# Adjacent weight rows a partition and regrouped attention outputs in a two-layer decode step

## The chip, the cores and the metric

The kernel runs on one core of a Trainium2 chip. The core has a matrix engine (PE, with its weight loads listed as PEld), a vector engine (DVE), a scalar engine (ACT), GpSimd (POOL), a queue engine that issues the loads (SP), and sixteen DMA engines that carry them. The metric is device time in microseconds of one execution, and a version of the kernel is judged by the median of several. Before the change the median of three runs is 268.01 us; the three lie between 267.9 and 269.52.

## The reference

Two layers that share all weights are run on four batch rows of one token each. Each layer is attention over a cache, then a gated feed-forward block, both behind a layer norm and added to the residual.

```python
def _A_ref(x, k_cache, v_cache, wq, wo):          # x: 4 x 1 x 512
    q = (x @ wq).reshape(B, Sq, Hq, Dh)           # 32 query heads of 128
    k, v = repeat(k_cache, 4), repeat(v_cache, 4) # 8 key heads, 4096 positions
    p = softmax(einsum(q, k) * Dh ** -0.5)
    return (p @ v).reshape(B, Sq, Hq * Dh) @ wo   # wo: 4096 x 512
def _B_ref(x, w_gate, w_up, w_down):              # 512 x 1792, 1792 x 512
    return (gelu(x @ w_gate) * (x @ w_up)) @ w_down

x = x + _A_ref(layernorm(x), ...); x = x + _B_ref(layernorm(x), ...)
x = x + _A_ref(layernorm(x), ...); x = x + _B_ref(layernorm(x), ...)
```

All tensors are bf16. The key and value caches are 33.5 MB each for the four batch rows. Keys are read once and serve both layers; most values are read twice, some tiles stay on the chip between the layers.

## The kernel before

**Stages.** `attend_first` does the first layer's attention of batch row 0, `dense_first` its feed-forward block. Then, for each following row, `attend` works on two rows at once: the second layer's attention of the row before and the first layer's attention of its own row. `dense` does the feed-forward block of one row. At the end `attend_last` does the second layer's attention of the last row, and `dense_last` does the second feed-forward block for all four rows together. The order of the instructions is written out by hand (`tc.manual_schedule()`), and each engine runs its own in that order.

**Loads.** All of them are issued by SP on one queue. A key or value tile is 512 KB: 128 partitions of 16 cache positions (4 KB). In batch row 0 the first four heads are loaded whole, 1 MB with 8 KB a partition. Value tiles go through a ring of eight slots (`VRing`); a slot is free again when PE has used its tile, and SP waits for that. `load_wq` brings the query weights, one half for each group of four key heads; `load_rest` (L158 to L171) brings the output weights in four pieces, then gate, up and down. Before the change the row of `wo`, gate and up that lands in partition p of block k is row 128k + p of the matrix, so that each row is a run of its own: 1 KB for the output weights, 3.5 KB for gate and up. Down already comes as two adjacent rows a partition.

**Heads.** Eight key heads form two groups (`gx`, `gy`) of four; each serves four query heads (`rep`). Odd batch rows begin with the second group. `Values.step` multiplies one value tile with the softmax weights on PE. Where a head is `streamed`, DVE turns the sums from PSUM (`turn_v`, L799) and adds them up (`sum_v`, L806 and L807); else L680 scales them. `hold=True` leaves that for a later `flush`. The results stand in `OT_bf`, `OL_bf` (the last head of the first layer) or `OT2_bf` (second layer, all four rows): 128 partitions, one column for each query head.

**Output projection.** Most of it goes through `RowProj.heads` (L405), where the attention output is the stationary operand and a row block of `wo_sb` streams by, four heads at once in four quarters of the array. `RowProj.split` (ACT L412, DVE L413) takes the sums out of PSUM, and `onto` adds them into the bank of `OutProj`, which does the heads that come last with `wo_sb` as the stationary operand (L275). `heads = pairs(...)` lists the four pairs of key heads in the order in which they are finished. `busy` issues matmuls whose result nobody reads.

**The end.** In `attend_last` the value tiles 0 to 7 of the second group come last. Its step is: four tiles, two pairs of heads of `rows`, two tiles, the third pair, `split`, one tile, `proj` for one head, one tile, `onto`, `proj` for the last head. `dense_last` then takes the residual into rows through a matmul with the identity (`row`, L1440).

```python
vals.step(4)
rows.heads(heads[0], hp)
rows.heads(heads[1], hp)
vals.step(2)
rows.heads(heads[2], hp)
rows.split()
```

Of the kernel before, what the change touches and what calls it, by code (L numbers as in the profile page):

```python
# [15 lines left out]
P = 128  # L16

LN_EPS = 1e-5
QD = 4
# [12 lines left out]
ROWS_A = 8  # L32
UP_ROWS = 8


@with_exitstack
def kernel(
# [111 lines left out]
    def cache_tile(cache, b, kvh, t):  # L149
        if whole(b, kvh):  # L150
            return cache[b, kvh].rearrange("(p t c) d -> t p c d", t=NT, p=P)[t]
        return cache[b, kvh].rearrange("(t p c) d -> t p c d", t=NT, p=P)[t]

    def load_wq(g):
        n = HG * Dh
        dq.dma_start(out=wq_sb[g][:], in_=wq_dram[:, :, g * n:(g + 1) * n])

    def load_rest():  # L158
        n = Hq // 4
        for i in range(4):  # L160
            dq.dma_start(out=wo_sb[:, i * n:(i + 1) * n], in_=wo_dram[:, i * n:(i + 1) * n])  # L161
        dq.dma_start(out=wg_sb[:], in_=B_w_gate.rearrange("(k p) n -> p k n", p=P))
        dq.dma_start(out=wu_sb[:], in_=B_w_up.rearrange("(k p) n -> p k n", p=P))
# [110 lines left out]
    def mac(dst, lhsT, rhs, first, last):  # L274
        nc.tensor.matmul(dst, lhsT=lhsT, rhs=rhs, start=first, stop=last, skip_group_check=True)  # L275
# [51 lines left out]
    def down_rows(H_bf):  # L327
        return streamed("y2", KD, [(H_bf[:, c, :1], wd_sb[:, c]) for c in range(KF)])

# [46 lines left out]
    class OutProj:  # L376
# [8 lines left out]
        def heads(self, h0, n):  # L385
            for i in range(h0, h0 + n):
                for k in range(KD):
                    mac(self.full[:, k], wo_sb[:, i, k * P:(k + 1) * P],
                        wide(self.o(i), self.width),
                        self.n == 0 and k == 0, self.n == Hq - 1)  # L390
                self.n += 1

    class RowProj:
# [23 lines left out]
        def onto(self, proj):  # L417
            for x in self.parts:
                for k in range(KD):
                    mac(proj.full[:, k], x[:, k * P:(k + 1) * P], wide(self.pick, proj.width),  # L420
                        False, False)
# [63 lines left out]
    def down(nb, H_bf, whole):  # L485
        y = acc([KD, WIDE], "y2", whole)
        for c in range(KF):
            for k in range(KD):
                mac(y[:, k], wd_sb[:, c, k * P:(k + 1) * P], wide(H_bf[:, c, :]),
                    c == 0 and k == 0, c == KF - 1)  # L490
        return y[:, :, :nb]
# [318 lines left out]
    class Values:  # L810
        def __init__(self, layer, b, tiles, prob, dst, keeps=(), streamed=(), paired=(), sums=None, park=(),
                     last_bank=None, off_ot=False, last_width=WEIGHT):
# [71 lines left out]
        def unit(self, kvh):  # L884
            pair = [2 * (kvh // 2), 2 * (kvh // 2) + 1]
            alone = kvh in self.streamed and kvh not in self.paired
            return [kvh] if self.tiles[-1][0] in pair or alone else pair

        def scale(self, ot, unit, rden):
            n, s = len(unit), unit[0] % GH  # L890
            if unit[0] in self.streamed:
# [67 lines left out]
    def attend_first():  # L959
# [7 lines left out]
                      streamed=[h for h in range(Hkv) if h != last],  # L967
                      paired=[h for h in range(Hkv) if h // 2 != last // 2])
        ring.extend(1, b, one(b))
        load_wq(gx)  # L970
        keys.load_heads(GH)
        load_wq(gy)
# [5 lines left out]
        for k in range(KD):  # L978
            nc.tensor.transpose(xT_ps[:, k, :], x_bf[:B, k * P:(k + 1) * P], ident_bf[:B, :B])
        nc.vector.tensor_copy(out=xb[:, :, :B], in_=xT_ps[:])  # L980
# [3 lines left out]
        def q_first(g):  # L984
# [6 lines left out]
            center(q1_bf[:, g], q[:, :, :B], t, rstd1, B)  # L991

        q_first(gx)
        q_build(q1_bf[:, gx, :, b])
        sc1 = new_scores()
        for s in range(GH):
            keys.turn(NT)
            for t in range(NT):
                scores_of(sc1, gx, [(s, t)])
# [18 lines left out]
        prob1[gy] = (soft_swap(p0), soft_recip(soft_den(p0)))  # L1018
        vals.step(TG)
        assert vals.left() == 0  # L1020
        load_rest()
# [113 lines left out]
    def attend(b, qy, before, norm, early=None):  # L1135
# [13 lines left out]
                       sums={4: (ps_sc, "sc"), 5: (ps_sm, "sm"), 6: (ps_sc, "sc")},  # L1149
                       last_bank=lambda: ps_sm.tile([P, 2, WEIGHT], FP32, name="ot", tag="sm"))  # L1150

# [62 lines left out]
        vals1.step(3)  # L1214
        scores(sc1, gy, 1, last_alone)
        p0 = soft(sc1)
        vals1.step(3)
# [14 lines left out]
        vals1.step(2)  # L1232
        rows.heads(heads[1], hp)
        vals1.step(1)
        proj = OutProj(o1(b), 1)
        spare = proj.bank[:, KD * WEIGHT:]
        rows.heads(heads[2], rep)
        busy(3, spare)
        vals1.step(1)
        rows.heads(heads[2] + rep, rep)  # L1240
        rows.split()
        busy(5, spare)
        vals1.step(1)
        proj.heads(heads[3], rep)
        vals1.step(1)
        assert vals1.left() == 0
        rows.onto(proj)
        proj.n = Hq - rep
        proj.heads(heads[3] + rep, rep)
        return proj.y, late2  # L1250

    def attend_last(q_bf, norm, before, late):
# [7 lines left out]
                      paired=[h for h in range(Hkv) if h // 2 != tiles[-1][0] // 2],  # L1260
                      last_width=WIDE)
        sc2 = [new_scores(early=True)]
# [26 lines left out]
        for part in full:  # L1289
            nothing(part[:])  # L1290
        nc.scalar.preload_act_table_set("gelu_apprx_tanh_and_others")
        vals.step(4)
        rows.heads(heads[0], hp)
        rows.heads(heads[1], hp)
# [77 lines left out]
    def dense_last(y, full, squares):  # L1372
# [65 lines left out]

        def row(to, k, lhsT, rhs):
            nc.tensor.matmul(to[k * QS:k * QS + B], lhsT=lhsT, rhs=rhs, start=False, stop=True,  # L1440
                             skip_group_check=True)

        for x in (xb[:], xlo):
            for k in range(KD):
                row(xr, k, x[:, k, :B], ident_bf[:])

# [126 lines left out]
```

## Time and profile before

| what | value |
|---|---|
| median of three runs | 268.01 us (267.9 to 269.52) |
| profiled execution | 268.99 us |
| its span | 267.2 us |
| mean granted clock of PE | 0.866 of full speed |
| PE busy | 195.1 us, 73% of the span |
| DVE busy | 182.2 us, 68% |
| ACT busy | 66.0 us, 25% |
| DMA | 30732 packets, 103.05 MB, 386 GB/s in the mean |
| share of sixteen DMA engines taken by SP's loads | 95.7% |

The span is the profiled execution from its first to its last instruction; its own time is 1.8 us longer. Times of the timeline count from the start of the span. A wait in brackets behind a row is the time for which the engine stood idle just before it, with what ended it.

### The profile page before, as it was taken

How to read it: one execution, taken by the hardware profiler on the slowest of the kernel's cores; microseconds unless marked ns; L12 is line 12 of the kernel's file. 1: busy time of each engine (PE TensorE's matmuls, PEld its weight loads, DVE VectorE, ACT ScalarE, POOL GpSimd, SP SyncE). 2: the span in 40 equal slices, each digit the busy share in tenths (PEclk: the TensorE clock that was granted, in tenths of full speed). 3: DMA queues.
4: the chain of work that ended last, by engine and by line, in shares of the span. 5: the costliest groups of instructions: out<-in, count | busy, mean ns of one | idle time of the engine just before them, and what ended most of it. 6: DMA issues, size and time to landing. Idle time of an engine off the chain costs nothing.

```text
span 267.2 us, 8596 instructions
## 1 busy us (share of the span) xinstructions
PE 195.1 (73%) x3767; PEld 114.8 (43%) x3775; DVE 182.2 (68%) x448; ACT 66.0 (25%) x136; POOL 3.9 (1%) x10
## 2 busy tenths in 40 slices
PE   1396246544689796989678968787788687888884
PEld 1333123322255453557436245464363354553563
DVE  3385955451335899884776998746769996568773
ACT  1001001100222422032323520304136103044642
POOL 2000000000001000000000000000000000000001
PEclk9998555655597959799999985899999979999999
DMA  7999999999994999999999999999999999999940
GB/s 244 432 416 421 423 429 417 408 385 406 413 412 177 394 416 417 420 417 400 390 414 416 416 419 421 416 415 375 403 418 418 421 415 418 420 405 405 413 160 3
DMA packets 30732, 103.05 MB, mean 386 GB/s; under 512 B 2788, under 2 KB 7144, under 8 KB 29672
## 3 DMA queue, kind: packets, MB, share of 16 engines
q1 hardware_dynamic: 30672, 102.51, 95.7%
q8 instruction: 29, 0.48, 0.6%
q14 instruction: 7, 0.06, 0.1%
q10 hardware_dynamic: 24, 0.01, 0.0%
HBM read 102.50 MB, written 0.00 MB: 384 GB/s over the span
## 4 chain that ended last, share of the span: by engine, by line
DMA 51%; PE 21%; DVE 16%; SPq 6%; ACT 3%; issue 3%; DVEq 0%
DMA v_t<-in_A_v_cache_dram 25%; DMA kp<-in_A_k_cache_dram 8%; DMA kw<-in_A_k_cache_dram 8%; PE sc L592 6%; DMA wu_sb<-in_B_w_up_dram 5%; DMA kw<-in_A_v_cache_dram 4%; SPq L161 4%; DVE kp L537 3%; PE ot L859 3%; DVE kw L537 3%; PE y L275 3%; PE so L791 2%; PE q L309 1%; DVE q L315 1%; DVE qb L360 1%
## 5 line engine op out<-in xcount | busy, mean ns | idle before, releaser
L592 PE MATMUL sc<-kw,qb 128*32 128x512 bf16 x244 | 39.6, 446 | 5.2 <-DVE kw L537 2.2
L592 PE MATMUL sc<-kp,qb 128*32 128x512 bf16 x268 | 40.1, 450 | 1.0 <-DVE kp L537 0.2
L592 PEld LDWEIGHTS <-qb 128*32 128x32 bf16 x512 | 23.1, 104 | 39.6 <-issue 21.4
L537 DVE STREAM_TRANSPOSE kw<-kw 128x1024 f32<-128x1024 f32 x32 | 38.0, 1215 | 0.7 <-DMA kw<-in_A_k_cache_dram 0.6
L537 DVE STREAM_TRANSPOSE kp<-kp 128x1024 f32<-128x1024 f32 x32 | 36.7, 1199 | 0.0
L859 PE MATMUL ot<-pe,v_t 128*128 128x32 bf16 (+1 forms) x896 | 30.0, 184 | 5.6 <-DMA v_t<-in_A_v_cache_dram 2.8
L859 PEld LDWEIGHTS <-v_t 128*128 128x128 bf16 x896 | 27.7, 100 | 13.7 <-issue 7.4
L614 ACT ACTIVATE pe<-sc,nl 128x512 bf16<-128x512 f32 x8 | 5.5, 687 | 85.9 <-DVE pe L611 67.6
L791 PE MATMUL so<-v_t,pe 128*32 128x256 bf16 x304 | 15.0, 319 | 13.6 <-DMA v_t<-in_A_v_cache_dram 11.6
L799 DVE STREAM_TRANSPOSE so<-so 128x512 f32<-128x512 f32 (+1 forms) x23 | 13.8, 599 | 11.1 <-PE so L791 11.1
L791 PEld LDWEIGHTS <-pe 128*32 128x32 bf16 x320 | 9.1, 105 | 19.4 <-issue 12.5
L602 DVE TENSOR_REDUCE pe<-sc 128x1 f32<-128x512 f32 x12 | 8.3, 691 | 9.2 <-PE sc L592 9.1
L405 PE MATMUL yr<-wo_sb,OT_bf 128*2 128x512 bf16 (+1 forms) x120 | 10.7, 425 | 4.9 <-DMA wo_sb<-in_A_wo_dram 4.9
L647 PE MATMUL x<-pe,ident_bf 128*32 128x128 bf16 x192 | 5.4, 233 | 11.8 <-DVE pe L622 11.8
L647 PEld LDWEIGHTS <-ident_bf 128*32 128x32 bf16 x256 | 5.3, 100 | 16.1 <-issue 14.1
L791 PE MATMUL so<-v_t,pl 128*32 128x256 bf16 x192 | 9.4, 275 | 3.3 <-DMA v_t<-in_A_v_cache_dram 3.3
L650 ACT CAST pe<-x 128x512 bf16<-128x512 f32 x12 | 7.0, 586 | 17.4 <-PE x L647 17.4
L275 PE MATMUL q<-xb,wq_sb 128*128 128x5 bf16 (+1 forms) x192 | 5.7, 173 | 6.5 <-DMA wq_sb<-in_A_wq_dram 6.5
L353 PE MATMUL qe<-q_bf,ident_bf 128*32 128x16 bf16 (+1 forms) x272 | 5.7, 176 | 5.6 <-DVE q_bf L335 2.9
L622 DVE STREAM_TRANSPOSE pe<-pe 128x512 bf16<-128x512 bf16 x12 | 8.4, 696 | 1.1 <-ACT pe L614 1.1
L275 PEld LDWEIGHTS <-wo_sb 128*128 128x128 bf16 x160 | 7.6, 101 | 3.3 <-DMA wo_sb<-in_A_wo_dram 2.6
L482 PEld LDWEIGHTS <-ident_bf 128*128 128x128 bf16 x63 | 5.2, 99 | 8.7 <-issue 4.3
(172 smaller groups left out, 255.2 us busy)
## 6 DMA issues: line engine op xcount, KB each, us to landing
v_t<-in_A_v_cache_dram SPq DMA_DIRECT2D x89, 512.0 KB, 8.5
kp<-in_A_k_cache_dram SPq DMA_DIRECT2D x32, 512.0 KB, 9.9
kw<-in_A_k_cache_dram SPq DMA_DIRECT2D x24, 512.0 KB, 9.6
wq_sb<-in_A_wq_dram SPq DMA_DIRECT2D x2, 2048.0 KB, 7.7
kw<-in_A_k_cache_dram SPq DMA_DIRECT2D x4, 1024.0 KB, 11.6
v_t<-in_A_v_cache_dram SPq DMA_DIRECT2D x4, 1024.0 KB, 14.2
wo_sb<-in_A_wo_dram SPq DMA_DIRECT2D x4, 1024.0 KB, 12.0
wq_sb<-in_A_v_cache_dram SPq DMA_DIRECT2D x3, 1024.0 KB, 11.8
```

Of the source, the lines that this page charges most:

```text
L161: dq.dma_start(out=wo_sb[:, i * n:(i + 1) * n], in_=wo_dram[:, i * n:(i + 1) * n])
L275: nc.tensor.matmul(dst, lhsT=lhsT, rhs=rhs, start=first, stop=last, skip_group_check=True)
L405: nc.tensor.matmul(self.rows[j:j + x.shape[1]], lhsT=x, rhs=wo_sb[:, i], start=self.n < QD, stop=True, skip_group_check=True)
L537: nc.vector.transpose(out=words, in_=words)
L592: nc.tensor.matmul(sc[s * QS:(s + 1) * QS], lhsT=qb[:, w0:w0 + 2 * W], rhs=kt[:, :, be // 2, :, be % 2], start=(t == 0 and be == 0), stop= ...
L602: nc.vector.tensor_reduce(out=m, in_=sc.rearrange("p c j -> p (c j)"), axis=AX.X, op=ALU.min if norm else ALU.max)
L622: nc.vector.transpose(out=flat, in_=flat)
L647: nc.tensor.matmul(x[a * QS:(a + 1) * QS, s], lhsT=ident_bf[:, s * QS:(s + 1) * QS], rhs=pT[:, a], start=True, stop=True, skip_group_check ...
L650: nc.scalar.copy(out=pe, in_=x.rearrange("p s t c h -> p (s t c h)"))
L791: nc.tensor.matmul(ps[d, :NW * QS], lhsT=x[:, w:w + NW].rearrange("p c h -> p (c h)"), rhs=v[:, i:i + NW, d], start=first and i == 0, stop ...
L799: nc.vector.transpose(out=flat, in_=flat)
L859: nc.tensor.matmul(self.ot[:, s % 2], lhsT=v[:, i, :], rhs=wide(pe[:, s, t * CH + i, :], self.ot.shape[-1]), start=(done == 0 and i == 0), ...
```

## The change

The rows of a weight matrix that land in one partition become adjacent rows in memory.

- Gate and up: partition p of a pair of blocks holds rows 2p and 2p + 1 of 256, so a run is 7 KB. The layout of the model dimension in `xb` and `XX` follows: block k holds every other element of a range of 256 (`every_other`). So the query weights are loaded by pairs too (two DMAs for each half, with the same 4 KB runs), and everything that writes this dimension takes every other column: the transposes of x, the output projection, `onto`, down. In `dense_last` the residual's rows are put back in natural order by 16 matmuls of 64 columns instead of 8 of 128.
- Output weights: the piece of key heads 4 and 5 (`QUADS`) is loaded as four adjacent rows a partition, a run of 4 KB. Its contraction index is then ordered otherwise, so the attention output of these eight query heads is reordered: `Values.regroup` does 16 matmuls with every fourth column of the identity into a PSUM bank that is no longer needed, and ACT copies the result back. It is called in all four attentions of the first layer and in `attend_last`, once the two heads are finished. In the third batch row these heads are the third pair, and the end of `attend` is written in another order there (`late_unit`).
- The first load is now one key head; the first half of the query weights comes behind it, and the head's two tiles are turned before the first queries.
- In `attend_last` the first pair of heads of `rows` comes ahead of four value tiles, and the table load of ACT behind the regrouping.

```diff
-    wq_dram = A_wq.rearrange("(k p) n -> p k n", p=P)
+    wq_dram = A_wq.rearrange("(k p e) n -> p k e n", p=P, e=2)
...
+    def by_quads(kvh):
+        return kvh // 2 == QUADS
+
+    def by_pairs(w):
+        return w.rearrange("p (k e) n -> p k e n", e=2)
+
+    def every_other(k):
+        lo = k // 2 * 2 * P + k % 2
+        return slice(lo, lo + 2 * P - 1, 2)
+
     def load_wq(g):
         n = HG * Dh
-        dq.dma_start(out=wq_sb[g][:], in_=wq_dram[:, :, g * n:(g + 1) * n])
+        for k in range(KD // 2):
+            dq.dma_start(out=by_pairs(wq_sb[g][:])[:, k], in_=wq_dram[:, k, :, g * n:(g + 1) * n])
...
+        wo_quads = A_wo.rearrange("(i p j) n -> p i j n", p=P, j=QD)
+        to_quads = wo_sb.rearrange("p (i j) n -> p i j n", j=QD)
+        for kvh in range(0, Hkv, 2):
+            if by_quads(kvh):
+                dq.dma_start(out=to_quads[:, kvh:kvh + 2], in_=wo_quads[:, kvh:kvh + 2])
+            else:
+                i = kvh * rep
+                dq.dma_start(out=wo_sb[:, i:i + n], in_=wo_dram[:, i:i + n])
+        dq.dma_start(out=by_pairs(wg_sb[:]),
+                     in_=B_w_gate.rearrange("(k p e) n -> p k e n", p=P, e=2))
+        dq.dma_start(out=by_pairs(wu_sb[:]),
+                     in_=B_w_up.rearrange("(k p e) n -> p k e n", p=P, e=2))
...
-                    mac(self.full[:, k], wo_sb[:, i, k * P:(k + 1) * P],
+                    mac(self.full[:, k], wo_sb[:, i, every_other(k)],
...
+        def regroup(self):
+            if not self.due:
+                return
+            kvh, n = self.due[0][1][0], sum(len(unit) for _, unit in self.due)
...
+            for j in range(QD):
+                for h in range(rep):
+                    nc.tensor.matmul(turned[h * QS:(h + 1) * QS, :, j], lhsT=ident_bf[:, j::QD],
+                                     rhs=o[:, :, h], start=True, stop=True, skip_group_check=True)
+            nc.scalar.copy(out=o, in_=turned)
...
+        keys.load_heads(1)
         load_wq(gx)
-        keys.load_heads(GH)
+        keys.load_heads(GH - 1)
         load_wq(gy)
...
+        late_unit = by_quads(heads[2] // rep)
+        if late_unit:
+            middle, end = (heads[1] + rep, rep), (heads[2], hp)
+            rows.heads(heads[1], rep)
...
+        if late_unit:
+            vals1.regroup()
+            busy(3, spare)
+            vals1.step(1)
+        rows.heads(*end)
         rows.split()
...
+        if late_unit:
+            proj.heads(heads[3] + rep, rep // 2)
+            rows.onto(proj)
+            proj.heads(heads[3] + rep + rep // 2, rep // 2)
...
+        rows.heads(heads[0], hp)
+        vals.step(4)
+        vals.regroup()
         nc.scalar.preload_act_table_set("gelu_apprx_tanh_and_others")
-        vals.step(4)
-        rows.heads(heads[0], hp)
         rows.heads(heads[1], hp)
         vals.step(2)
...
         for x in (xb[:], xlo):
             for k in range(KD):
-                row(xr, k, x[:, k, :B], ident_bf[:])
+                half = slice(k % 2 * P // 2, (k % 2 + 1) * P // 2)
+                for e in range(2):
+                    row(xr, k, x[:, k // 2 * 2 + e, :B], ident_bf[:, half], slice(e, P, 2))
```

More of the change, by code (lines that the diff above doesn't have):

```diff
@@ L327, in down_rows @@
     def down_rows(H_bf):
-        return streamed("y2", KD, [(H_bf[:, c, :1], wd_sb[:, c]) for c in range(KF)])
+        return streamed("y2", KD, [(H_bf[:, c, :1], wd_sb[:, c]) for c in range(KF)], adjacent)
     def q_tile():
@@ L1232, in attend @@
         vals1.step(2)
[L1233 removed]
+        late_unit = by_quads(heads[2] // rep)
+        if late_unit:
+            middle, end = (heads[1] + rep, rep), (heads[2], hp)
+            rows.heads(heads[1], rep)
+        else:
+            middle, end = (heads[2], rep), (heads[2] + rep, rep)
+            rows.heads(heads[1], hp)
         vals1.step(1)
@@ L1236, in attend @@
         spare = proj.bank[:, KD * WEIGHT:]
-        rows.heads(heads[2], rep)
+        rows.heads(*middle)
         busy(3, spare)
         vals1.step(1)
-        rows.heads(heads[2] + rep, rep)
+        if late_unit:
+            vals1.regroup()
+            busy(3, spare)
+            vals1.step(1)
+        rows.heads(*end)
         rows.split()
-        busy(5, spare)
-        vals1.step(1)
+        if not late_unit:
+            busy(5, spare)
+            vals1.step(1)
         proj.heads(heads[3], rep)
```

50 lines of the change are left out of this document (32 added, 18 removed).

## The prediction

> **What bounds the kernel now.** I read the page first, then the windows of 4 us, then stretches of the timeline. The page's span, its rates in 40 slices of 6.7 us, and the chain that ended last:
>
> ```profile
> span 267.2 us, 8596 instructions
> GB/s 244 432 416 421 423 429 417 408 385 406 413 412 177 394 416 417 420 417 400 390 414 416 416 419 421 416 415 375 403 418 418 421 415 418 420 405 405 413 160 3
> DMA 51%; PE 21%; DVE 16%; SPq 6%; ACT 3%; issue 3%; DVEq 0%
> ```
>
> The loads set the time: 102.5 MB (the page's HBM line) stream at about 415 GB/s from the third microsecond to the 258th. Only three things add to that: one hole (177 in the thirteenth slice, and 412 ahead of it), shallow dips, and a tail of pure compute. The windows put numbers on it (busy time of PE, PEld, DVE, ACT, POOL; then granted clock, DMA share, GB/s):
>
> ```profile
> 0.00:4.00 4.00, 0.85 (x20) 0.68 (x20) 1.84 (x14) 1.28 (x1) 0.70 (x6) 1.00 0.54 126
> 8.00:12.00 4.00, 2.16 (x80) 1.98 (x80) 1.14 (x6) 0.00 (x0) 0.00 (x0) 1.00 1.02 430
> 28.00:32.00 4.00, 1.10 (x18) 0.89 (x18) 4.00 (x6) 0.59 (x1) 0.00 (x0) 0.50 1.04 425
> 56.00:60.00 4.00, 1.26 (x12) 0.33 (x16) 3.02 (x7) 0.00 (x0) 0.00 (x0) 0.50 1.09 386
> 64.00:68.00 4.00, 2.46 (x40) 2.21 (x40) 1.16 (x4) 0.15 (x1) 0.00 (x0) 0.50 1.02 417
> 156.00:160.00 4.00, 1.66 (x46) 1.29 (x46) 3.85 (x11) 1.67 (x4) 0.00 (x0) 0.78 1.04 420
> 160.00:164.00 4.00, 3.91 (x71) 2.18 (x68) 4.00 (x5) 0.00 (x0) 0.00 (x0) 0.50 1.02 417
> 184.00:188.00 4.00, 3.15 (x104) 1.97 (x101) 2.41 (x9) 0.81 (x1) 0.00 (x0) 1.00 0.98 353
> ```
>
> A ramp of 126 GB/s; 430 while whole key heads come in 8 KB packets, 425 with key tiles in 4 KB packets, 417 with gate and up in 3.5 KB packets; 386 while the output weights come in 1 KB packets; 353 where the value ring runs thin. So an edit counts if it makes a packet cheaper, deepens a dip, or lengthens the tail after the last load.
>
> **The change, part by part.**
>
> *Loads.* The output weights come in four pieces of 1.05 MB. When each has landed is read off the first PE row that waits for it (start, duration, what, wait in brackets):
>
> ```profile
> 59.76 1.02 PE L405 MATMUL yr<-wo_sb,OT_bf 128*2 128x512 bf16 x8 [1.68 <-DMA wo_sb<-in_A_wo_dram]
> 62.44 1.02 PE L405 MATMUL yr<-wo_sb,OT_bf 128*2 128x512 bf16 x8 [1.65 <-DMA wo_sb<-in_A_wo_dram]
> 69.59 0.61 PE L482 MATMUL g<-wg_sb,ident_bf 128*128 128x512 bf16 x1 [1.71 <-DMA wg_sb<-in_B_w_gate_dram]
> 73.94 0.93 PE L1323 MATMUL u<-wu_sb,xb 128*8 128x448 bf16 x16 [0.40 <-DMA wu_sb<-in_B_w_up_dram]
> ```
>
> The second and the third piece land 2.68 us apart, 391 GB/s. The quarter of heads 4 to 7's first pair would come as 256 packets of 4 KB instead of 1024 of 1 KB; at the 417 of the windows that is 2.51 us, a gain of 0.17 (0 to 0.24, the latter at 430). Up lands 4.35 us after gate, 422 GB/s for 1.84 MB. Rows in pairs make 7 KB packets; at 430 each matrix gains 0.08, together 0.16 at most, and since 8 KB and 4 KB packets differ by 1% in the windows I take 0.1. Loads together: -0.3, bounds -0.4 and 0. What lands earlier before the hole moves the hole as a whole, because the loads after it wait for a chain that begins with up; so the gain is kept.
>
> The Trainium skill has a rule here (DMA: Bandwidth & Descriptors, "Why small descriptors are slow"): about 3 cycles of overhead for each packet, beside one 32-byte beat per cycle. As an estimate by that page, 35 cycles for 1 KB against 131 for 4 KB would save the quarter 0.17 us and the pairs 0.12, also about 0.3; it speaks against a larger gain from the 7 KB packets.
>
> *The first load of one key head.* The bytes up to the second group's query weights stay the same, the order differs; SP issues two DMAs more. The wait in which the start ends:
>
> ```profile
> 37.00 1.04 PE L791 MATMUL so<-v_t,pe 128*32 128x256 bf16 x16 [7.90 <-DMA v_t<-in_A_v_cache_dram]
> ```
>
> One head (1.05 MB, 2.4 us at 430) moves ahead of the query weights, so the first queries come 2.4 us later, while two key transposes run earlier. Whatever remains is covered: PE waits 7.9 us for the first value load at 37.00. The two issues more on SP stand behind data already queued, under the same cover; without it they would be paid in full. Cost 0; the ramp of the first 4 us may change with the first packets, which no row shows: bounds -0.3 and +0.3, value 0.
>
> *Every other column.* Weights taken with a step of two, and down's rows through `adjacent`. The groups by form:
>
> ```profile
> L275 PEld LDWEIGHTS <-wo_sb 128*128 128x128 bf16 x160 | 7.6, 101 | 3.3 <-DMA wo_sb<-in_A_wo_dram 2.6 <-issue 0.7
> L275 PEld LDWEIGHTS <-wu_sb 128*128 128x128 bf16 x24 | 0.7, 97 | 0.2 <-issue 0.2
> L309 PE MATMUL q<-wq_sb,xb 128*32 128x512 bf16 x112 | 7.7, 382 | 0.3 <-DVE xb L425 0.3
> L309 PE MATMUL g<-wg_sb,xb 128*32 128x448 bf16 x48 | 2.8, 354 | 0.0
> ```
>
> L1430 already takes `wu_sb` by every other column: 97 ns a load against 101 for packed `wo_sb`. Gate's rows already use `adjacent`: 354 ns for 448 columns, query's contiguous ones 382 for 512; 64 columns at 0.42 ns are the difference. Cost 0, bounds 0 and 0.1. In `dense_last` the residual takes 16 narrower matmuls instead of 8; PE idles 0.40 us right behind them, which hides them:
>
> ```profile
> 263.18 0.95 PE L1440 MATMUL yo<-wd_sb,wq_sb 128*4 128x128 bf16 x56 [0.40 <-DVE wq_sb L1460]
> ```
>
> *Regrouping.* 16 small matmuls and an ACT copy. Nearest rows: 16 matmuls of the query sums, and a small ACT copy:
>
> ```profile
> 243.21 0.27 PE L353 MATMUL qe<-q_bf,ident_bf 128*32 128x16 bf16 x16 [0.21 <-DVE q_bf L335]
> 262.84 0.27 ACT L1464 COPY wq_sb<-xr 128x128 f32<-128x128 f32 x1
> ```
>
> So 0.3 us of PE, then about 0.3 until the copy is read. It has four places. In the first batch row, PE waits for values right behind it; in the second and the fourth, PE waits for the softmax a little later:
>
> ```profile
> 51.84 0.62 PE L791 MATMUL so<-v_t,pe 128*32 128x256 bf16 x8 [0.61 <-DMA v_t<-in_A_v_cache_dram]
> 116.94 0.41 PE L647 MATMUL x<-pe,ident_bf 128*32 128x128 bf16 x16 [0.78 <-DVE pe L622]
> ```
>
> 0.61 and 0.78 us of idle PE hide 0.3. Without that cover 0.3 each would be paid. The ACT copy stands ahead of the exponential there, which first waits for DVE's maximum: cost 0.
>
> *Third batch row.* Heads 4 and 5 are late here, so their 8 row matmuls move behind the first tile of the last head, ahead of the split. The end of that row now:
>
> ```profile
> 177.57 0.75 DVE L413 SCALAR_TENSOR_TENSOR yt<-yt,masks,yr 128x512 bf16<-128x512 bf16 x1
> 177.94 1.09 PE L275 MATMUL y<-OT_bf,wo_sb 128*128 128x64 bf16 x16
> 179.55 0.17 DVE L680 TENSOR_TENSOR OL_bf<-ot,rden 128x16 bf16<-128x16 f32 x1 [1.23 <-PE ot L859]
> 179.78 0.65 PE L275 MATMUL y<-OL_bf,wo_sb 128*128 128x64 bf16 x16
> 186.20 0.40 PE L791 MATMUL so<-v_t,pl 128*32 128x256 bf16 x8 [0.48 <-DMA v_t<-in_A_v_cache_dram]
> ```
>
> 8 row matmuls take 0.44 (the tail's 16 in 1.04 against 8 in 0.60, quoted below). They push the projection at 177.94 and the tile behind it by 0.44, so L680 could start at 179.99 instead of 179.55; the split, whose DVE part now starts at 177.57, comes after them (cast 0.59, then 0.75) and ends at about 180.0 too. L680 runs at 180.0, the last projection from 180.25, and the four matmuls of `onto` between its halves add 0.1: y about 0.55 later. Queued behind it are the value tiles whose use frees ring slots, and SP's next loads wait for those slots, in the very stretch that runs at 353 GB/s. But PE waits there for data (0.48 us at 186.20), so part is absorbed: I take +0.3, bounds 0 and +0.6.
>
> *The tail.* The last value tiles, with the waits in brackets:
>
> ```profile
> 253.58 0.18 DVE L807 TENSOR_TENSOR OT_bf<-ov,rden 128x8 bf16<-128x8 f32 x1
> 253.83 1.06 PE L791 MATMUL so<-wq_sb,pl 128*32 128x256 bf16 x32 [0.36 <-ACT pl L650]
> 254.71 1.04 PE L405 MATMUL yr<-wo_sb,OT_bf 128*4 128x512 bf16 x16
> 254.94 0.73 DVE L799 STREAM_TRANSPOSE so<-so 128x512 f32<-128x512 f32 x1
> 255.84 0.34 PEld L791 LDWEIGHTS <-pl 128*32 128x32 bf16 x16 [0.59 <-DMA wq_sb<-in_A_v_cache_dram]
> 255.97 0.18 DVE L807 TENSOR_TENSOR OT_bf<-ov,rden 128x8 bf16<-128x8 f32 x1
> 256.29 0.60 PE L405 MATMUL yr<-wo_sb,OT_bf 128*4 128x512 bf16 x8
> 256.94 0.59 ACT L412 CAST yt<-yr 128x512 bf16<-128x512 f32 x1 [1.21 <-PE yr L405]
> 258.32 0.27 PEld L859 LDWEIGHTS <-kw 128*128 128x128 bf16 x8 [0.21 <-DMA kw<-in_A_v_cache_dram]
> 258.95 0.55 PE L275 MATMUL y<-OT_bf,wo_sb 128*128 128x32 bf16 x16
> ```
>
> Now the two pairs of row matmuls (254.71, 1.04 us) fill PE while DVE turns and sums heads 4 and 5 (254.94 to 256.15, 1.21 us). After the change the first pair goes ahead: it needs the sums of 253.58 to 253.76, so it runs from 253.85 and pushes the four value tiles to 254.3, ending at 255.35. Then comes the regrouping, whose matmuls wait for DVE's 1.21 us: **PE stands still** from 255.35 to about 256.65, with the second pair, two tiles and everything else queued behind in order. From there: regrouping to 256.9, second pair 0.44, two tiles 0.43 (half of the 1.06 at 253.83 less about 0.2 of drain), third pair 0.44, so the rows end at about 258.3 instead of 256.89. The split's cast (0.59; ACT's table load, now behind the copy, may hold it by some tenths) and its DVE part (0.75) end between 259.7 and 259.9. Three blocks of 0.43 on PE (a tile, four heads' projection, a tile) end at 259.6. L680 follows the split on DVE, and the last projection starts at about 260.15, not 258.95: **+1.2**. Bounds: +0.4, if the 0.8 us that PE now waits for the last loads (0.59 at 255.84, 0.21 at 258.32) all serve as cover; +1.6, if the whole step from 256.89 to 258.3 and some tenths more reach the end.
>
> **Sum:** -0.3 + 0 + 0.3 + 1.2 = +1.2 us. The profiled execution took 268.99 us, its span 267.2 and 1.8 around it; it would be 270.2. It stands 1.0 above the median of the three runs shown (268.01; they reach from 267.9 to 269.52), so the median becomes **269.2**.
>
> **The rivals.**
> *The tail's wait is covered, the loads end last.* For it: the two waits for DMA in the tail. Against: the stall comes first and in-order work piles up behind it. -0.3 + 0 + 0.4 gives 268.1.
> *The start gains too.* The ramp at 126 GB/s improves with 8 KB packets in front and the tail is covered: -0.4 - 0.3 + 0 gives 267.3.
> *The clock falls in the tail* (the slower side). At 156 us PE was quiet for about two microseconds and the granted clock fell to 0.50: the two windows above. [...] Some 5 us of PE work then remain; at half clock, half of it on the path, +2.5: 271.7.
> The Trainium skill (TensorE: Matmul & The Clock Gate, on the HAM clock gate) asks for an idle window of about 3.4 us before the clock is halved; the trace shows it after a shorter quiet stretch, so the rule alone does not exclude this rival.
> *The packets do not merge.* Then the page would count as many packets as before, and -0.3 is missing: 269.5.
>
> **How the numbers follow.** Forecast 0.52, covered tail 0.25, start gains 0.08, clock 0.10, no merging 0.05. The range 267.2 to 270.8 holds all but the clock, with the bounds of tail and third row added (269.2 + 0.4 + 0.3 + 0.3 = 270.2, and some 0.6 for the spread of the runs). One per cent, 2.7 us, is about what a measurement of this kernel tells from no change: faster by more 0.02 (of the start), within 0.85, slower by more 0.13 (the clock, and 0.03 of the forecast).
>
> **What would show it.** Packets on the page fall from 30732 by 1280 to 29452. The third piece of the output weights lands about 2.5 us after the second. In the tail PE idles some 1.3 us ahead of the regrouping, released by DVE's sums, and the first row matmuls stand before four value tiles. The last projection starts about 2 us after the last load landed, not 0.6. Wrong, if the regrouping finds its sums ready, if the slices around the third row's dense layer change by more than 1 us, or if the hole changes its length.

## The result

The changed kernel takes **271.51 us** (median of six runs, 270.92 to 272.5) against 267.95 for the kernel before (six runs): a ratio of 1.0125, 95% interval 1.009 to 1.016, so 2.4 to 4.3 us slower. The prediction said 269.2, with a range from 267.2 to 270.8: the loss is larger than forecast. The profiled execution of the changed kernel took 271.61 us, 0.1 above its median, and its span is 269.8. By the profiled executions the change costs 2.6 us, by the medians 3.6, because the profiled execution of before was 1.0 above its median.

The page of the changed kernel: span, GB/s in 40 slices, packets, and the chain that ended last.

```profile
span 269.8 us, 8779 instructions
...
GB/s 252 376 418 421 421 426 419 410 399 414 412 405 210 403 415 419 416 417 414 356 404 415 420 418 418 418 417 356 403 414 416 418 420 418 415 386 390 414 89 4
DMA packets 29486, 103.07 MB, mean 382 GB/s; under 512 B 2820, under 2 KB 6152, under 8 KB 28424
...
DMA 39%; DVE 25%; PE 23%; SPq 5%; ACT 4%; issue 3%; DVEq 0%
```

There are 1246 packets fewer than before (30732), so the merging took place. The loads still set the time, but DMA's share of the chain fell from 51% to 39%. What does not fit the forecast stands in the second slice: 376 GB/s where 432 ran.

**The start.** Two windows of the changed kernel (busy times of PE, PEld, DVE, ACT, POOL; granted clock, DMA share, GB/s), then its first wait for values:

```profile
4.00:8.00 4.00, 0.57 (x16) 0.48 (x16) 2.15 (x7) 0.00 (x0) 1.02 (x1) 1.00 0.97 335
6.00:9.00 3.00, 0.00 (x0) 0.00 (x0) 2.44 (x3) 0.00 (x0) 0.47 (x1) 1.00 0.95 287
```

```profile
37.81 1.04 PE L811 MATMUL so<-v_t,pe 128*32 128x256 bf16 x16 [7.84 <-DMA v_t<-in_A_v_cache_dram]
```

The same stretch of the kernel before:

```profile
6.00:9.00 3.00, 0.52 (x19) 0.52 (x20) 0.00 (x0) 0.00 (x0) 0.00 (x0) 1.00 1.04 434
```

Between 6 and 9 us the engines are nearly as busy (a share of 0.95 against 1.04) and move 287 GB/s instead of 434: each packet takes longer. PE still waits 7.84 us for the first value load, as long as before, and the load itself lands 0.81 us later (37.81 against 37.00).

**The loads of weights.** The landings in the changed kernel, by the PE rows that wait for them:

```profile
57.88 1.02 PE L425 MATMUL yr<-wo_sb,OT_bf 128*2 128x512 bf16 x8 [1.62 <-DMA wo_sb<-in_A_wo_dram]
60.59 1.02 PE L425 MATMUL yr<-wo_sb,OT_bf 128*2 128x512 bf16 x8 [1.69 <-DMA wo_sb<-in_A_wo_dram]
63.13 1.02 PE L425 MATMUL yr<-wo_sb,OT_bf 128*2 128x512 bf16 x8 [1.52 <-DMA wo_sb<-in_A_wo_dram]
65.84 1.10 PE L295 MATMUL y<-OT_bf,wo_sb 128*128 128x64 bf16 x16 [1.68 <-DMA wo_sb<-in_A_wo_dram]
```

The third piece, the one in four rows, lands 2.54 us after the second; its neighbours in 1 KB rows take 2.71 each. That is 0.17, the figure of the forecast. The Trainium skill (DMA: Bandwidth & Descriptors, "Why small descriptors are slow") gave the same 0.17 as an estimate from its overhead per packet; the trace agrees.

**The third batch row**, where the regrouping stands in another order:

```profile
176.82 0.17 ACT L926 CAST OT_bf<-so 128x8 bf16<-128x8 f32 x1 [4.44 <-PE so L924]
178.04 0.60 PE L425 MATMUL yr<-wo_sb,OT_bf 128*2 128x512 bf16 x8
...
178.58 1.10 PE L295 MATMUL y<-OT_bf,wo_sb 128*128 128x64 bf16 x16
...
179.37 0.75 DVE L433 SCALAR_TENSOR_TENSOR yt<-yt,masks,yr 128x512 bf16<-128x512 bf16 x1 [1.83 <-ACT yt L432]
...
180.19 0.17 DVE L700 TENSOR_TENSOR OL_bf<-ot,rden 128x16 bf16<-128x16 f32 x1
...
181.34 0.17 DVE L445 TENSOR_TENSOR xb<-XX,y 128x4 bf16<-128x4 f32 x1 [0.97 <-PE y L295]
```

The eight row matmuls behind the tile start at 178.04 and their split is over at 180.12 instead of 178.32 (177.57 and 0.75, quoted in the prediction). L700 now follows the split rather than the tile, 0.64 later than before (179.55), and the result of the layer enters the residual at 181.34.

**The tail.** The changed kernel's last value tiles:

```profile
254.75 0.18 DVE L827 TENSOR_TENSOR OT_bf<-ov,rden 128x8 bf16<-128x8 f32 x1
...
254.98 0.60 PE L425 MATMUL yr<-wo_sb,OT_bf 128*4 128x512 bf16 x8 [0.35 <-ACT pl L670]
255.41 1.05 PE L811 MATMUL so<-wq_sb,pl 128*32 128x256 bf16 x32
...
257.54 0.18 DVE L827 TENSOR_TENSOR OT_bf<-ov,rden 128x8 bf16<-128x8 f32 x1
257.76 0.30 PE L924 MATMUL so<-OT_bf,ident_bf 128*32 128x8 bf16 x16 [1.31 <-DVE OT_bf L827]
...
258.32 1.28 ACT L1358 ACT_TABLE_LOAD   x1
...
258.76 0.62 PE L425 MATMUL yr<-wo_sb,OT_bf 128*4 128x512 bf16 x8
...
259.61 0.59 ACT L432 CAST yt<-yr 128x512 bf16<-128x512 f32 x1
...
261.17 0.55 PE L295 MATMUL y<-OT_bf,wo_sb 128*128 128x32 bf16 x16
```

PE stands still for 1.31 us ahead of the regrouping, released by DVE's sums. From the sums at 254.75 to the last projection at 261.17 it takes 6.42 us; before, from 253.58 to 258.95, it took 5.37. The tail is 1.05 longer, and the other 1.17 of the shift came in ahead of it. PE no longer waits for the last loads here; before, it waited for the last of them at 258.32, and the last projection started 0.63 behind that.

### The profile page after: what moved, and what is told of

It is laid out like the page before. It is cut to its first block, busy times and chain, and to the rows that moved or that the text cites. A ratio compares the mean times of both kernels' runs of the same rounds, so it can differ in the third digit from the quotient of the medians.

```text
span 269.8 us, 8779 instructions
## 1 busy us (share of the span) xinstructions
PE 191.9 (71%) x3853; PEld 114.2 (42%) x3861; DVE 182.3 (68%) x448; ACT 66.8 (25%) x141; POOL 3.9 (1%) x10
## 4 chain that ended last, share of the span: by engine, by line
DMA 39%; DVE 25%; PE 23%; SPq 5%; ACT 4%; issue 3%; DVEq 0%
DMA v_t<-in_A_v_cache_dram 26%; DMA kp<-in_A_k_cache_dram 8%; DVE kp L557 7%; PE sc L612 6%; DVE kw L557 6%; DMA wg_sb<-in_B_w_gate_dram 5%; PE ot L880 5%; PE y L295 3%; PE so L811 2%; SPq L179 2%; SPq L176 1%; DVE q L335 1%; PE q L329 1%; SPq L168 1%; DVE pe L622 1%
## 5 line engine op out<-in xcount | busy, mean ns | idle before, releaser
L612 PE MATMUL sc<-kw,qb 128*32 128x512 bf16 x244 | 37.5, 442 | 3.6 <-DVE qb L380 2.0
L612 PE MATMUL sc<-kp,qb 128*32 128x512 bf16 x268 | 37.5, 428 | 1.0 <-DVE kp L557 0.2
L612 PEld LDWEIGHTS <-qb 128*32 128x32 bf16 x512 | 21.7, 102 | 35.6 <-issue 18.1
L295 PEld LDWEIGHTS <-wq_sb 128*128 128x128 bf16 x192 | 5.5, 101 | 9.9 <-DMA wq_sb<-in_A_wq_dram 9.8
```

The lines of the kernel that those rows point to most:

```text
L612: nc.tensor.matmul(sc[s * QS:(s + 1) * QS], lhsT=qb[:, w0:w0 + 2 * W], rhs=kt[:, :, be // 2, :, be % 2], start=(t == 0 and be == 0), stop= ...
```

## The experiments

The theory after this first look: the time went into the tail and the third row, and the start matters by at most 0.3 us. The rival: the first load itself loses about 0.9 us. All ratios are to the kernel before on the same chip, whose medians there are 268.66 to 268.77 us, so 0.1% is 0.27 us.

### One part undone at a time

**start_back**: the first half of the query weights ahead of four key heads again.

```diff
-        keys.load_heads(1)
         load_wq(gx)
-        keys.load_heads(GH - 1)
+        keys.load_heads(GH)
...
-        keys.turn(NT)
         q_first(gx)
...
```

> The changed kernel with one part undone: query weights come first again, then the four key heads, and the first head's tiles are turned behind the first queries. My theory (the time went into the tail and the third row) gives the changed kernel's time, 271.5 us, less at most 0.3. The rival, that the first load itself loses what the windows from 6 to 9 us show (319, 213 and 328 GB/s instead of 418 to 451, about 0.9 us of loads), gives 270.7 or less, and then the stretch from 4 to 12 us should run at about 425 GB/s again.

Measured: 272.11 us, ratio 1.0129 (1.0082 to 1.0177), no better than the change (1.0125). The first value load lands at 38.96, and the slow stretch has moved to the front: 294 GB/s from 4 to 8 us against 428 before. It follows the query weights, and the key head is not its cause. So this edit did not take the start's loss away, and it can't tell the theory from the rival.

**tail_back**: the tail's order of before, with the regrouping behind both pairs of heads.

```diff
-        rows.heads(heads[0], hp)
-        vals.step(4)
-        vals.regroup()
         nc.scalar.preload_act_table_set("gelu_apprx_tanh_and_others")
+        vals.step(4)
+        rows.heads(heads[0], hp)
         rows.heads(heads[1], hp)
+        vals.regroup()
```

> The changed kernel with the tail in the old order: table load, four value tiles, two pairs of row matmuls, and the regrouping only behind them, where its sums are ready. My theory (PE stands still for 1.31 us while DVE turns and sums heads 4 and 5, and the end moves by 1.05 of it) gives 0.7 to 1.1 us less than the changed kernel, about 270.5. The rival (the last loads end the tail whatever PE does) gives no difference, 271.5.

Measured: 270.98 us, 1.0077 (1.004 to 1.0114), 0.48% below the change's 1.0125. In this order only a part of the tail's loss goes: the profile still has 6.22 us from the sums (254.66) to the last projection (260.88). It shows a wait for DVE's sums and an idle stretch of PE without a visible cause:

```profile
257.27 0.30 PE L924 MATMUL so<-OT_bf,ident_bf 128*32 128x8 bf16 x16 [0.44 <-DVE OT_bf L827]
...
259.99 0.23 PE L295 MATMUL y<-OT_bf,wo_sb 128*128 128x32 bf16 x3 [0.50 <-issue]
```

This profiled execution (272.13 us) was the slowest of the six.

**third_back**: no regrouping in the third batch row, and its order of before; this leaves out the reordering of heads 4 and 5 there.

```diff
-        late_unit = by_quads(heads[2] // rep)
+        late_unit = False
```

> The changed kernel with the third batch row's end in the old order and without its regrouping (this leaves out the reordering of heads 4 and 5 in the first layer's attention of that row). My theory of a row that ends 0.87 us later and a value ring that passes part of it on gives 0.4 to 1.0 us less than the changed kernel, about 270.8. The rival (absorbed by waits for data in the dense layer) gives 271.5.

Measured: 270.88 us, 1.0078 (1.0044 to 1.0112), 0.47% below the change. In its profile the sums that stood at 254.75 stand at 253.87, 0.88 earlier, and from there the tail takes 6.43 us again.

**no_quads**: no quarter in four rows, no regrouping, and the tail and the third row in their old order. Pairs and the key head in front stay.

```diff
     def by_quads(kvh):
-        return kvh // 2 == QUADS
+        return False
...
```

> The changed kernel without the quarter as four rows: no regrouping anywhere, the third row and the tail in the old order; pairs of rows and the first key head stay. If the tail (1.05) and the third row (0.4 to 1.0) are most of the loss, this gives 269.6 to 270.2; if the pairs or the first load carry the loss, 271 or more; if these cost nothing, 268.0.

Measured: 269.57 us, 1.0037 (1.0006 to 1.0067). So the four rows and their regrouping cost most of it, and something that has nothing to do with them costs about 1 us. This kernel's first value load lands at 38.00, and 6 to 9 us runs at 269 GB/s.

### What is slow at the start

Three things can make the query weights slow: adjacent rows in a partition, two DMAs instead of one, or the key head in front. These kernels take them apart.

**wq_split**: the kernel before, its query weights in two DMAs, with the old rows.

```diff
-        dq.dma_start(out=wq_sb[g][:], in_=wq_dram[:, :, g * n:(g + 1) * n])
+        for k in range(0, KD, 2):
+            dq.dma_start(out=wq_sb[g][:, k:k + 2], in_=wq_dram[:, k:k + 2, g * n:(g + 1) * n])
```

> The kernel before, with each half of the query weights loaded by two DMAs (blocks 0 and 1, then blocks 2 and 3); rows in the old layout, one per partition and block. Theory A (the slow stretch of the start comes from pairs of adjacent rows in one load): no slow stretch, first value wait at 37.0, time as before within 0.15%. Rival B (it comes from the split in two DMAs): 200 to 330 GB/s for some 3 us while the first half arrives, first value wait near 38, time 0.3 to 0.4% above before.

Measured: 270.3 us, 1.0061 (1.0038 to 1.0085), more than the rival's 0.3 to 0.4%. The first value load lands at 38.47. This contradicts the theory that pairs of adjacent rows are slow. Its window:

```profile
4.00:8.00 4.00, 0.40 (x11) 0.27 (x8) 0.82 (x5) 0.00 (x0) 1.02 (x1) 1.00 1.00 305
```

**wq_odd**: no_quads, with the even and the odd rows as the two DMAs. Every row lands where it did.

```diff
-        for k in range(KD // 2):
-            dq.dma_start(out=by_pairs(wq_sb[g][:])[:, k], in_=wq_dram[:, k, :, g * n:(g + 1) * n])
+        for e in range(2):
+            dq.dma_start(out=by_pairs(wq_sb[g][:])[:, :, e], in_=wq_dram[:, :, e, g * n:(g + 1) * n])
```

> No regrouping and no quads, one key head first, pairs in gate, up and query weights, but the two DMAs of a half of the query weights take the even and the odd rows instead of the two ranges of 256 rows: the rows land in the same places, and no DMA brings two adjacent rows. Theory A (adjacent rows within a DMA): no slow stretch at 6 to 9 us, first value wait at 37.0 to 37.2, time 0.1% below to 0.1% above before. Rival B (two DMAs): slow stretch stays, 0.3 to 0.4% above before.

Measured: 268.95 us, 1.0007 (0.9984 to 1.0029), first value load at 36.72, 419 GB/s from 6 to 9 us. Two DMAs as such are not slow either. What sets this kernel apart from no_quads and from wq_split is how far one DMA reaches: over all four blocks of 1 MB of the matrix here, over two adjacent ones there.

**head_first**: the kernel before with the key head in front, nothing else.

```diff
+        keys.load_heads(1)
         load_wq(gx)
-        keys.load_heads(GH)
+        keys.load_heads(GH - 1)
...
+        keys.turn(NT)
         q_first(gx)
...
```

> The kernel before, with the first load of one key head and its two tiles turned before the first queries; nothing else. Theories A and B: no slow stretch, the query weights run at 410 to 450 GB/s, first value wait at 37.0 to 37.4, time within 0.15% of before. Rival C (any load of query weights behind a key head is slow): 200 to 330 GB/s at 6 to 9 us, first value wait near 38, 0.3 to 0.4% above before.

Measured: 268.09 us, 0.9981 (0.9949 to 1.0014), first value load at 36.80, 419 GB/s from 6 to 9 us. By itself this part costs nothing that can be measured.

**wq_late**: no_quads, with three key heads ahead of the query weights.

```diff
-        keys.load_heads(1)
+        keys.load_heads(GH - 1)
         load_wq(gx)
-        keys.load_heads(GH - 1)
+        keys.load_heads(1)
```

> No regrouping and no quads, pairs in gate, up and query weights, but three key heads are loaded ahead of the first half of the query weights. Theory A: the slow stretch moves with the query weights to 12 to 16 us, first value wait near 38, 0.3 to 0.4% above before. Rival D (the pairs are slow only in the first 10 us, while something else of the start runs): no slow stretch at 12 to 16 us and none before; the first value wait comes at 37.0, 0 to 0.1% above before, unless the queries, 5 us later than with one head first, use up the cover of 7.9 us.

Measured: 269.5 us, 1.0029 (1.0001 to 1.0056), first value load at 38.26. The slow stretch moved with the load: 412 GB/s from 6 to 9 us, and then

```profile
10.00:13.00 3.00, 0.00 (x0) 0.00 (x0) 0.00 (x0) 0.00 (x0) 0.00 (x0) 1.00 0.92 279
```

So it belongs to the transfer and not to a time in the start. The expectation had it move with the load, but to 12 to 16 us, and by a wrong reason: adjacent rows, which wq_split takes away.

**gy_first**: no_quads, with the second group's query weights ahead of the first's, both behind the one key head. All kernels above load the first group's half first, and the second group's half, later, at full rate.

```diff
         keys.load_heads(1)
+        load_wq(gy)
         load_wq(gx)
         keys.load_heads(GH - 1)
-        load_wq(gy)
```

> No quads; pairs, one key head first, then the query weights of the second group, then those of the first (in all runs so far the first group's came first), two DMAs of 256 rows each as in the change. Theory 1 (the first visit to these 2 MB of the matrix is slow, whichever columns it takes): 200 to 330 GB/s while the second group's half arrives, at 6 to 9 us, and 400 or more for the first group's half behind it. Theory 2 (the columns of the first group are slow): 400 or more at 5 to 8 us, 200 to 330 GB/s behind it. First value wait at 38 either way, 0.3 to 0.5% above before.

Measured: 269.64 us, 1.0034 (1.0 to 1.0068), first value load at 37.96. Its windows:

```profile
6.00:9.00 3.00, 0.00 (x0) 0.00 (x0) 2.44 (x3) 0.00 (x0) 0.41 (x1) 1.00 0.94 284
10.00:13.00 3.00, 0.00 (x0) 0.00 (x0) 0.00 (x0) 0.00 (x0) 0.00 (x0) 1.00 1.02 421
```

The first 3 MB are the key head and the second group's half, which is slow now; the first group's half behind it runs at 421. Whichever half of the columns comes first has the slow stretch.

**wq_cross**: the kernel before, two DMAs with the old rows again, but blocks 0 and 2, then 1 and 3.

```diff
-        dq.dma_start(out=wq_sb[g][:], in_=wq_dram[:, :, g * n:(g + 1) * n])
+        for k in range(KD // 2):
+            dq.dma_start(out=wq_sb[g][:, k::2], in_=wq_dram[:, k::2, g * n:(g + 1) * n])
```

> The kernel before with each half of the query weights loaded by two DMAs, this time blocks 0 and 2, then blocks 1 and 3; rows in the old layout. If what is slow is a DMA that stays within one half (2 MB) of the matrix: each of these reaches over 3 MB, so no slow stretch, first value wait at 36.7 to 37.1, ratio 0.998 to 1.001. If two DMAs in the old layout are slow whichever blocks they take (so that only even and odd rows escape): 200 to 330 GB/s at 3 to 7 us, first value wait at 38.4, ratio 1.004 to 1.008, as with blocks 0 and 1.

Measured: 268.33 us, 0.999 (0.9967 to 1.0013), first value load at 36.72. The window beside that of wq_split, from which only the choice of blocks differs:

```profile
4.00:8.00 4.00, 0.77 (x17) 0.61 (x17) 0.82 (x5) 0.00 (x0) 1.02 (x1) 1.00 1.05 430
```

430 against 305 GB/s with the same number of DMAs, bytes and packets of 4 KB.

**Only the first of the two DMAs is slow.** PE waits for each of them. The rows of the changed kernel, then those of wq_split:

```profile
9.23 0.22 PE L295 MATMUL q<-xb,wq_sb 128*128 128x5 bf16 x2 [4.66 <-DMA wq_sb<-in_A_wq_dram]
11.71 1.82 PE L295 MATMUL q<-xb,wq_sb 128*128 128x5 bf16 x62 [2.27 <-DMA wq_sb<-in_A_wq_dram]
```

```profile
7.83 0.21 PE L276 MATMUL q<-xb,wq_sb 128*128 128x5 bf16 x2 [3.60 <-DMA wq_sb<-in_A_wq_dram]
10.28 1.81 PE L276 MATMUL q<-xb,wq_sb 128*128 128x5 bf16 x62 [2.23 <-DMA wq_sb<-in_A_wq_dram]
```

The second DMA, 1.05 MB as well, lands 2.48 and 2.45 us behind the first, 423 and 428 GB/s. The first lands 2.00 us later in wq_split than in wq_cross (5.83). The second one stays within a half of the matrix too, the other one, and no DMA has been there before it. So a short reach is not slow in itself: what is slow here is the first DMA on the matrix where it is confined to the first 2 MB.

### Closing the sum

**after_odd**: the changed kernel with even and odd rows as its two DMAs, the edit of wq_odd.

```diff
-        for k in range(KD // 2):
-            dq.dma_start(out=by_pairs(wq_sb[g][:])[:, k], in_=wq_dram[:, k, :, g * n:(g + 1) * n])
+        for e in range(2):
+            dq.dma_start(out=by_pairs(wq_sb[g][:])[:, :, e], in_=wq_dram[:, :, e, g * n:(g + 1) * n])
```

> The changed kernel, with one difference: the two DMAs of a half of the query weights take the even and the odd rows, not the two ranges of 256 rows; every row lands where it did. Theory (a DMA that stays within 2 MB of the matrix is slow the first time, and costs the changed kernel 0.3 to 0.5% at its start): no stretch below 350 GB/s at 6 to 9 us, first value wait at 36.7 to 37.0 instead of 37.81, ratio to before 1.007 to 1.010 instead of 1.0125. Rival (the loss at the start is covered later, the regrouping costs it all): 1.0125 as before.

Measured: 270.7 us, 1.0059 (1.0027 to 1.0092), first value load at 36.73, 419 GB/s from 6 to 9 us. The ratio lies a little below the expected band. The tail is untouched, so it has to show the same loss, and it does:

```profile
252.77 0.18 DVE L827 TENSOR_TENSOR OT_bf<-ov,rden 128x8 bf16<-128x8 f32 x1
...
255.79 0.30 PE L924 MATMUL so<-OT_bf,ident_bf 128*32 128x8 bf16 x16 [1.31 <-DVE OT_bf L827]
...
259.20 0.55 PE L295 MATMUL y<-OT_bf,wo_sb 128*128 128x32 bf16 x16
```

The stall is 1.31 us again, and from the sums to the last projection it takes 6.43.

**all_back**: after_odd with the edits of tail_back and third_back (leaves out the reordering of heads 4 and 5 in the third row).

```diff
-        late_unit = by_quads(heads[2] // rep)
+        late_unit = False
...
-        rows.heads(heads[0], hp)
-        vals.step(4)
-        vals.regroup()
         nc.scalar.preload_act_table_set("gelu_apprx_tanh_and_others")
+        vals.step(4)
+        rows.heads(heads[0], hp)
         rows.heads(heads[1], hp)
+        vals.regroup()
```

> The changed kernel with even and odd rows in the loads of the query weights, the tail's order of before (table load, four tiles, both pairs of heads, then the regrouping) and no regrouping in the third batch row (leaves out the reordering of heads 4 and 5 there). Left of the change are the pairs, the quarter in four rows, one head first, and four regroupings. If start, tail and third row are all of the loss: ratio 0.998 to 1.001, last projection at 258.5 to 259.3 of the span. If a further cost stands in the other regroupings or the columns: 1.003 or more.

Measured: 268.97 us, 1.0011 (0.998 to 1.0041). Start, tail and third row are the loss within what the runs can tell; the interval also leaves room for a further cost of 0.4%. The profiled execution of this kernel (270.7 us) was slower than its median, and its last projection at 260.53 misses the expected 258.5 to 259.3. Its tail still takes 6.02 us from the sums, 0.65 more than before:

```profile
254.51 0.18 DVE L827 TENSOR_TENSOR OT_bf<-ov,rden 128x8 bf16<-128x8 f32 x1
...
257.15 0.30 PE L924 MATMUL so<-OT_bf,ident_bf 128*32 128x8 bf16 x16 [0.43 <-DVE OT_bf L827]
```

The old order can't hide DVE's sums wholly either (0.43), because its two pairs of heads do not last as long as DVE. But this wait does not set the end here. PE waits for the last loads again, as in the kernel before:

```profile
259.91 0.27 PEld L880 LDWEIGHTS <-kw 128*128 128x128 bf16 x8 [0.16 <-DMA kw<-in_A_v_cache_dram]
...
260.53 0.55 PE L295 MATMUL y<-OT_bf,wo_sb 128*128 128x32 bf16 x16
```

From the last load (259.91) to the last projection it takes 0.62, before 0.63. The last load came 5.40 after the sums, before 4.74, and that is the whole 0.65.

No version is faster than the kernel before by more than the runs can tell: head_first (0.9981) and wq_cross (0.999) have 1 in their intervals.

## Why the prediction was wrong

**What failed is the step "The first load of one key head", cost 0, bounds -0.3 and +0.3.** It counted two DMAs more on SP and called them covered by PE's 7.9 us of waiting for values. It put no price on the transfers themselves, although the diff splits each half of the query weights in two. And the cover was none: what PE waits for there is a load at the back of the same queue, so a stream that loses a microsecond delays that load, and PE waits as long as before (7.84). A wait for DMA covers work on an engine; it does not cover a slower DMA. The price, from the medians: without the four rows, the kernels with the slow stretch stand at 1.0037, 1.0061, 1.0029 and 1.0034 (no_quads, wq_split, wq_late, gy_first; mean 1.0040), those without it at 1.0007, 0.9981 and 0.999 (wq_odd, head_first, wq_cross; mean 0.9993). The difference is 0.47%, **1.3 us**, by the intervals of the seven ratios good to about 0.6 either way. In the traces the first value load lands at 37.81 to 38.96 in the eight kernels with it and at 36.72 to 37.00 in the six without. Not all of this delay is seen to last: in the means over the eight profiles without the four rows, the result of the first layer's attention comes 1.3 us later with the slow stretch in batch row 0 (68.55 against 67.23) and 0.7 later in the next row (125.41 against 124.71). The hole in the loads lies between the two. The prediction held that the hole moves as a whole with what lands before it; for this delay that is not seen, and what made up the rest is not shown.

**The tail, +1.2, was right:** +1.05 against the profile of before. The new order takes 6.42 or 6.43 in all four profiles that have it. The old one takes 4.96 to 7.44 in eight, as the last loads land early or late, so the 1.05 rests on the one profiled execution of before; the steps of the prediction, less that 1.17, were met within 0.2 each. The stall was forecast as 1.3 us from 255.35; it is 1.31 and, less the 1.17 by which the tail began later, starts at 255.28. The table load holds the split's cast by 0.23 (259.61, where the rows of 258.76 end at 259.38). PE's two waits for the last loads are gone, but gave little cover. By medians, third_back, which still has the tail's new order, stands 0.38% above the mean of the four kernels with the slow start and no four rows, 1.0 us.

**The third row, +0.3 with bounds 0 and 0.6, was undersized.** The late order delays the result by 0.87 (181.34 against 180.47), not 0.55: the split of the late pair ends at 180.12, about as forecast, but both halves of the last projection then queue around `onto`, and the addition waits 0.97 for them instead of 0.74. The row of before:

```profile
180.47 0.17 DVE L425 TENSOR_TENSOR xb<-XX,y 128x4 bf16<-128x4 f32 x1 [0.74 <-PE y L275]
```

The half that the thin ring was to absorb is not seen absorbed: the profile of third_back reaches the last sums 0.88 earlier. By medians tail_back, which keeps this order, stands 0.37% above the same mean, 1.0 us. But it keeps a part of the tail's loss too: all_back, with the same tail and without this order, stands 0.18% above the mean of the kernels without the slow stretch, 0.5 us. That leaves 0.5 to 1.0 for the third row; the intervals of such differences reach about 0.9 to either side, so 0.3 is not excluded.

**The loads, -0.3, were right:** the quarter gained its 0.17. Gate lands 4.25 to 4.29 us behind the last piece of the output weights in the ten profiles with pairs, 4.34 to 4.43 in the four with the old rows: the 0.1 of the forecast. Up shows no gain where PE waits for it: it lands 4.39 and 4.80 behind gate with pairs (wq_odd, wq_late), 4.35 and 4.38 with the old rows (before, head_first). The medians are too coarse for this: wq_odd, which has the pairs without the four rows, stands at 1.0007.

**Regrouping at no cost in the other rows was right.** All instructions of the line in the changed kernel, and what PE stood idle for ahead of them:

```profile
its engine sat idle before it (us, times) until:
  issue: 1.8, 2
  DVE OT_bf L827: 1.3, 1
```

Only one of the five places waits for sums, the tail's; the 1.8 of "issue" stands ahead of weight loads (PEld), not of matmuls. Every other column at no cost was right too: a load of the strided output weights takes 101 ns as before.

```profile
L295 PEld LDWEIGHTS <-wo_sb 128*128 128x128 bf16 x160 | 7.6, 101 | 3.8 <-DMA wo_sb<-in_A_wo_dram 2.6
```

**The rivals.** The clock in the tail did not fall: 1.00 in the window that follows the stall, so the slower rival came near the right time (271.7) by luck, through the wrong mechanism.

```profile
260.00:264.00 4.00, 3.59 (x110) 2.88 (x111) 2.55 (x11) 2.17 (x12) 0.78 (x1) 1.00 0.02 4
```

In the profile of tail_back it did fall, to 0.63 from 262 to 264 us, with no idle stretch of PE above 0.50 us from 256 us on. So single executions can lose time to a lower clock in the tail, and there it took no stall of 1.3 us. Packets merged, and the tail was not covered. The sum as measured: -0.3 for the loads, +1.3 for the start, +0.5 to +1.0 for the third row, +1.05 for the tail, together 2.6 to 3.1 us, inside the measured 2.4 to 4.3.

## What to carry to other kernels

When a load is split or its rows regrouped, price the transfer itself, and ask which part of the matrix each DMA covers: here the same bytes in the same packets cost 1.3 us more when the first DMA on the matrix stayed within half of it. Idle time of an engine that waits for a load is no cover for anything that slows the loads ahead of it in that queue. A reordering that waits for another engine's sums belongs behind work that lasts as long as those sums; where the last instructions leave no such work, a gain of 0.17 us in the load does not pay for it.

## What the runs showed of the hardware

In the start of the kernel, the first DMA on the query weights ran slowly when it took 4 KB out of each 8 KB row of the first 256 rows only (1 MB out of 2 MB). Windows of three to four microseconds that hold it show 243 to 305 GB/s (tail_back and wq_split), and single microseconds down to 176 (start_back), at a DMA share of 0.92 to 1.00 in the windows. The second DMA, over the other 256 rows, landed 2.45 to 2.50 us behind it in the seven kernels where PE waits for both, 419 to 428 GB/s. Windows of kernels whose first DMA reached over 3 or 4 MB show 419 to 430, and the second visit to the same rows, for the other columns, 421. Where in the start it stands, and which columns come first, does not matter.

The Trainium skill (DMA: Bandwidth & Descriptors, "Latency and other measured facts") lists row pitches of 2 to 8 MiB that lower the rate of a copy, at 4 MiB to about half, and calls aliasing of memory channels an inference that is not verified. Here the pitch from row to row is 8 KB in wq_split, which is slow, and in wq_cross, which is fast, and the second visit is fast at the same pitch, so that rule alone does not sort these runs. Why this first DMA is slow stays open. All slow kernels begin with the lower 256 rows, so no run tells whether these rows or the first access counts, nor a cost of first access from a clash of addresses.
